# Two chunks of the w3·w_out product in float32r from split parts, and a new order of batch 0's softmax among the weight conversions

## Chip, cores and metric

One core of a Trainium2 chip runs the kernel. The metric is the device time of one execution in microseconds; the time before is a median of three runs. All times inside a run come from one profiled execution, counted from the start of its span. TensorE is called PE, VectorE DVE, ScalarE ACT, SyncE SP.

## The reference

Eight batches, eight heads, 512 tokens and 32 state rows of 64 values each. Attention runs both ways, tokens over state rows and state rows over tokens, each with its own softmax; the two results are put below each other, and heads are laid side by side to rows of 512. Those 4,352 rows go through a bilinear layer:

```python
scores = scale * np.matmul(x, state.transpose(0, 1, 3, 2))
a = softmax(scores)                      # tokens: 512 x 32 a head
xread = np.matmul(a, state)
scores2 = scale * np.matmul(state, x.transpose(0, 1, 3, 2))
a2 = softmax(scores2)                    # state rows: 32 x 512 a head
sread = np.matmul(a2, x)
x = rows of xread and sread              # (8*544) x 512
h = (x @ w1) * (x @ w2) @ w3
out = h @ w_out
```

w1 and w2 are 512x1024, w3 is 1024x1024, w_out 1024x512. The weights come as float64.

## The kernel before

The two last products are joined: the kernel computes wo = w3 @ w_out once (1024x512) and then, for every row, (x@w1 * x@w2) @ wo. Since attention's result is a weighted sum of state rows, w1 and w2 are first multiplied by the state of each batch (per_head, L148); these products, split into a high and a low float32r part, are the `sw_hi` and `sw_lo` tiles. stage1_sums (L312) multiplies them with the attention weights `at_hi` and `at_lo` in three terms (lo·hi, hi·hi, hi·lo), hidden (L299) multiplies the two halves and splits the result into `g_hi` and `g_lo`, and stage2 (L339, L332) multiplies by wo. Batch 0 goes in this plain form; batches 1 to 7 go through quarter_batch (L518), which does the last product in quarters with combined weights; state_rows (L675) does the state rows at the end.

This case is about the prologue, in which the weights are loaded and turned into float32, and batch 0's softmax is computed beside it.

**Conversion.** to_f32 (L103) turns one tile of 128x1024 float64 into float32. SP loads it into `raw` (three places). ACT makes two passes: the high words (L119, into the output) and the low words (L127, into `ulps`, two places; in the first two chunks DVE does this, L123). After a `yield` DVE shifts (L131) and adds (L135). A load into a place of `raw` waits until ACT's second pass of the tile three loads earlier is done.

**Tiles in order.** Eight chunks `w34_k` (half w_out, half the first four row blocks of w3) are converted into places of `w_sb`; w34_first (L568) multiplies each into four PSUM sums, four float32 matmuls a chunk, which the profile shows as eight records. Tiles 4 to 7 of w3 (`convert_w3`, L576) follow, each for one further sum of eight float32 matmuls (w34, L580); their outputs `w3` have two places, so tile 6 waits until PE has used tile 4, and tile 7 until tile 5. finish (L561) splits a sum into wo: a cast on ACT (L98), a subtraction on DVE (L99). Eight halves of w1 and w2 are converted too (convert_half, L588): the first four before, the other four after the first stage1. The second four overwrite places that hold w_out.

**Batch 0's softmax** is the generator scores (L180): it is advanced with `go(softmax)` between conversions. Its steps before: the scores on PE; transposing (L191), the state side's maxima (L194, L195) and exponentials on ACT (L205, two, with their sums), the token side's maxima, subtraction and exponential (L214, L215, L218); the sums and reciprocals (L220 to L226); the transposing back and the split into `at` (L231); last the transposing of the state side's exponentials (L238) into the tile `work`, from which SP's sixteen DMAs of move_blocks (L168, L172) build the tile that read_state (L244) multiplies.

**What sets the order.** PE and SP issue in the order of the code all along. In the prologue, until `order.close()` (L643), ACT and DVE do too; behind it a scheduler places their instructions, those of hidden with priority. Each engine works through its instructions in order, so one that waits holds up all behind it. sets (L592) is two units of per_head for a quarter of the weights; a pair of PSUM banks (`two_banks`) has three places, taken in turn by the w34 pair, the scores of batch 0, the units, and the sums of stage 1.

Of the kernel before, what the change touches and what calls it, by code (L numbers as in the profile page):

```python
# [29 lines left out]
P = 128  # L30
# [6 lines left out]
PLAIN = 1  # L37

@with_exitstack
def attn_bilinear_kernel(  # L40
# [62 lines left out]
    def to_f32(pool, src, out, ends=(NW,), loads=(), wout=None):  # L103
# [12 lines left out]
        for part in parts:  # L116
# [4 lines left out]
            )  # L121
            if len(parts) > 1:
# [53 lines left out]
    def attention_steps(b):  # L176
# [3 lines left out]
        def scores():  # L180
# [15 lines left out]

            first, second = (maxima, turn) if b > PLAIN else (turn, maxima)
            with tc.issue_after(first().ins):
                second()
# [3 lines left out]
            for kt in range(KT):  # L203
                one = slice(kt, kt + 1)
                nc.scalar.activation(  # L205
                    out=e2[:, kt], in_=ps[:, kt], func=AF.Exp, bias=m2[:, one], scale=SCALE, accum_out=sum2[:, one]
                )
            if b > PLAIN:
                yield
# [4 lines left out]
            nc.vector.tensor_reduce(out=m1, in_=s1v, axis=AX.X, op=ALU.max)  # L214
            nc.vector.tensor_tensor(  # L215
                out=s1v, in0=s1v, in1=m1.unsqueeze(2).broadcast_to([P, J, NS]), op=ALU.subtract
            )
            nc.scalar.activation(out=s1, in_=s1, func=AF.Exp, scale=SCALE)  # L218
            yield
            nc.vector.tensor_scalar_add(sum2, sum2, 1e-9)  # L220
            nc.vector.reciprocal(out=sum2, in_=sum2)
# [9 lines left out]
            nc.vector.transpose(out=flat(at), in_=flat(s1))  # L231
            at_tiles[b] = [att.tile([P, KT, S], F32R, name=f"at_{part}", bufs=1) for part in ("hi", "lo")]
            last = split(*at_tiles[b], at)
            yield

# [317 lines left out]
    with tc.tile_pool(name="pro", bufs=2) as pro:  # L553
# [7 lines left out]
        def finish(i):  # L561
            split(wo["hi"][:, i], wo["lo"][:, i], w34_ps[i][:, :DO])

        def convert_first(k):
            ends = PARTS.get(k, (NW,))
            return to_f32(pro, w34_k[k], chunks[k], ends, (), wout=w_out[k])

        def w34_first(k):  # L568

            for i in range(FT // 2):  # L570
# [5 lines left out]
        def convert_w3(i):  # L576
            w3s[i] = pro.tile([P, NW], F32, name="w3", bufs=2)
            return to_f32(pro, w3t[i - FT // 2], w3s[i])
# [31 lines left out]
        for k in range(FT + AHEAD):  # L610
            run([partial(convert_first, k) if k < FT else partial(convert_w3, k - FT // 2)])
            if k >= AHEAD:
                w34_first(k - AHEAD)
        load_x(0)
# [137 lines left out]
```

## Time and profile before

| | |
|---|---|
| median of three runs | 491.09 us (490.76 to 491.37) |
| the profiled execution's own time | 490.61 us |
| its span, first to last instruction | 488.8 us |
| busy: PE, DVE, ACT | 481.6, 391.1, 235.3 us |
| bytes moved by DMA | 52.49 MB |
| mean granted PE clock | 1.000 |

A row of the timeline gives start, length, engine, line, operation, output and inputs, sizes and count; in brackets how long the engine was idle before it, and what released it. "PEld" is the loading of the stationary operand, "SPq" the issuing of DMAs by SP, "issue" time in which nothing visible was waited for. Matmuls overlap, so the interval between two starts tells more than a row's length. Some matmul records are missing in a trace.

### The profile page before, as it was taken

What the parts mean: (1) busy time and instruction counts of PE and PEld (TensorE: products, weight loads), DVE (VectorE), ACT (ScalarE), POOL (GpSimd) and SP (SyncE); (2) the same over time, 40 slices, a digit from 0 to 9 for tenths busy, and PEclk for the clock granted to TensorE, in tenths of its full rate; (3) what the DMA queues carried; (4) which work ended last, traced back from release to release, by engine and by line L of the source; (5) the groups of instructions that cost most, each with busy time, mean ns of one, the idle gap of its engine ahead of it and who ended that gap; (6) DMA issues with size and microseconds to landing.
All of it is one profiled execution on the core that took longest, in us unless ns stands there. A gap on an engine that the chain in (4) does not pass through costs nothing.

```text
span 488.8 us, 8607 instructions
## 1 busy us (share of the span) xinstructions
PE 481.6 (99%) x3390; PEld 368.9 (75%) x3390; DVE 391.1 (80%) x576; ACT 235.3 (48%) x364; POOL 0.2 (0%) x4
## 2 busy tenths in 40 slices
PE   8999999999999999999999999999999999999996
PEld 5444467768688878887888788877977797899885
DVE  5669897699999679958995899599859985678870
ACT  4777784453547044704570556055515541353640
POOL 0000000000000000000000000000000000000000
PEclk9999999999999999999999999999999999999999
DMA  8996981153105404130413041305230223001101
GB/s 341 356 365 251 370 306 27 17 205 90 21 6 196 108 9 171 43 99 4 180 39 94 4 181 41 90 5 180 44 87 5 89 47 84 6 2 43 45 1 44
DMA packets 56361, 52.49 MB, mean 107 GB/s; under 512 B 42752, under 2 KB 50944, under 8 KB 51712
## 3 DMA queue, kind: packets, MB, share of 16 engines
q1 hardware_dynamic: 47488, 43.27, 27.0%
q10 hardware_dynamic: 8832, 8.65, 5.2%
q8 instruction: 27, 0.44, 0.4%
q14 instruction: 14, 0.11, 0.1%
HBM read 38.27 MB, written 8.91 MB: 97 GB/s over the span
## 4 chain that ended last, share of the span: by engine, by line
PE 78%; DVE 11%; ACT 5%; DMA 3%; SPq 2%; issue 1%; ACTq 0%; DVEq 0%
PE ps L321 29%; PE ps_o L436 11%; PE ps L448 8%; PE ps L148 6%; PE ps_o L441 5%; PE ps L453 4%; PE ps L690 3%; PE ps_o L571 3%; PE ps L571 3%; PE ps_o L335 2%; SPq L172 2%; DMA raw<-in_w_dram 2%; PE ps L692 2%; ACT ulps L127 2%; PE ps_o L253 1%; DVE raw L383 1%
## 5 line engine op out<-in xcount | busy, mean ns | idle before, releaser
L321 PE MATMUL ps<-at_lo,sw_hi 128*128 128x512 f32 x256 | 101.3, 396 | 0.1
L321 PE MATMUL ps<-at_hi,sw_lo 128*128 128x512 f32 x256 | 99.8, 390 | 0.0
L321 PE MATMUL ps<-at_hi,sw_hi 128*128 128x512 f32 x256 | 99.7, 389 | 0.0
L525 ACT COPY tmp<-ps 128x512 f32<-128x512 f32 x56 | 32.8, 585 | 118.1 <-PE ps L321 118.1
L321 PEld LDWEIGHTS ps<-at_lo,sw_hi 128*128 128x128 f32 x256 | 48.1, 188 | 16.4 <-DVE g_lo L99 5.0
L321 PEld LDWEIGHTS ps<-at_hi,sw_lo 128*128 128x128 f32 x256 | 48.1, 188 | 10.3
L321 PEld LDWEIGHTS ps<-at_hi,sw_hi 128*128 128x128 f32 x256 | 48.1, 188 | 9.6 <-issue 0.2
L464 DVE TENSOR_TENSOR tmp<-tmp,ps 128x512 f32<-128x512 f32 x42 | 28.8, 687 | 18.4 <-PE ps L453 17.5
L405 DVE TENSOR_TENSOR g_x<-tmp,ps 128x512 f32<-128x512 f32 x28 | 18.9, 676 | 26.3 <-ACT tmp L525 26.3
L98 ACT CAST g_hi<-raw 128x512 fp32r<-128x512 f32 x42 | 24.6, 618 | 31.9 <-DVE raw L405 23.6
L99 DVE TENSOR_TENSOR sw_lo<-ps,sw_hi 128x1024 fp32r<-128x1024 f32 (+1 forms) x34 | 38.0, 1146 | 1.5 <-ACT sw_hi L98 1.5
L436 PEld LDWEIGHTS ps_o<-t,g_hi 128*128 128x128 f32 x224 | 27.8, 191 | 5.0 <-issue 5.0
L148 PE MATMUL ps<-w_sb,st 64*32 64x512 f32 (+1 forms) x544 | 31.4, 570 | 0.0
L98 ACT CAST sw_hi<-ps 128x1024 fp32r<-128x1024 f32 (+1 forms) x34 | 31.0, 967 | 0.1
L98 ACT CAST g_hi<-g_x 128x512 fp32r<-128x512 f32 x42 | 25.4, 626 | 11.3 <-DVE g_x L405 6.4
L436 PE MATMUL ps_o<-t,g_hi 128*128 128x256 f32 x224 | 29.7, 286 | 0.0
L99 DVE TENSOR_TENSOR g_lo<-raw,g_hi 128x512 fp32r<-128x512 f32 x42 | 27.9, 679 | 2.2 <-PE ps_o L441 1.6
L436 PE MATMUL ps_o<-wo,g_hi 128*128 128x256 f32 x224 | 29.1, 283 | 0.0
L436 PEld LDWEIGHTS ps_o<-wo,g_hi 128*128 128x128 f32 x224 | 28.3, 192 | 0.5
L584 PE MATMUL ps_o<-w_sb,w 128*128 128x512 f32 x64 | 28.5, 599 | 0.0
L99 DVE TENSOR_TENSOR g_lo<-g_x,g_hi 128x512 fp32r<-128x512 f32 x42 | 27.1, 681 | 1.8 <-PE ps_o L441 1.8
L448 PE MATMUL ps<-t,g_hi 128*128 128x512 f32 x112 | 28.0, 392 | 0.0
(103 smaller groups left out, 784.5 us busy)
## 6 DMA issues: line engine op xcount, KB each, us to landing
raw<-in_w_k_dram SPq DMA_DIRECT2D x8, 1024.0 KB, 6.8
x_d<-in_x_d_dram SPq DMA_DIRECT2D x8, 1024.0 KB, 6.8
raw<-in_w_dram SPq DMA_DIRECT2D x8, 1024.0 KB, 6.7
x_s<-in_x_s_dram SPq DMA_DIRECT2D x8, 1024.0 KB, 5.1
out_dram<-tmp ACTq DMA_DIRECT2D x56, 128.0 KB, 1.8
raw<-in_w3t_dram SPq DMA_DIRECT2D x4, 1024.0 KB, 7.4
e<-work SPq DMA_DIRECT2D x112, 32.0 KB, 2.0
sread<-turned SPq DMA_DIRECT2D x128, 4.0 KB, 1.7
```

What stands on the lines that cost most here:

```text
L98: nc.scalar.copy(out=hi, in_=src),
L99: nc.vector.tensor_tensor(out=lo, in0=src, in1=hi.bitcast(F32), op=ALU.subtract),
L148: nc.tensor.matmul(ps[j * NS:(j + 1) * NS, q], sts[b][rows, j], moving(rows, j), start=True, stop=True)
L321: nc.tensor.matmul(ps[:, i], w[:, kt, c:c + P], a[:, kt], start=(k == 0), stop=(k == 3 * KT - 1))
L436: nc.tensor.matmul(ps[:, tt * HO:(tt + 1) * HO], g, w(part, k), start=(fresh and k == 0 and tt == 0 and part == "lo"), stop=False, skip_gr ...
L441: nc.tensor.matmul(ps[:, tt * HO:(tt + 1) * HO], g, w("hi", k), start=False, stop=(k == QF - 1), skip_group_check=True)
L448: nc.tensor.matmul(ps[:, tt].rearrange("p (n d) -> p n d", n=2), g, w(k), start=(k == 0), stop=False, skip_group_check=True,)
L453: nc.tensor.matmul(ps[:, tt, :HO], g, w(k)[:, 0], start=False, stop=(k == QF - 1), skip_group_check=True)
L464: sum2 = lambda out, x, y: nc.vector.tensor_tensor(out=out, in0=x, in1=y, op=ALU.add)
L525: copied = nc.scalar.copy(out=a_sb, in_=ps[:, 0])
L571: nc.tensor.matmul(w34_ps[i][:, :DO], chunks[k][:, DO + i * P:DO + (i + 1) * P], w_out[k], start=(k == 0), stop=(k == FT - 1),)
L584: nc.tensor.matmul(w34_ps[i][:, :DO], w3s[i][:, k * P:(k + 1) * P], w_out[k], start=(k == 0), stop=(k == FT - 1))
```

## The change

Three edits of the prologue, all in the code that orders it.

First, chunks 4 and 6 (`SPLIT`) are multiplied in float32r: their two halves are split into high and low parts (`split_of`), into tiles of the `sw` pool, and w34_first makes three matmuls instead of one for each of the four sums. The split is called by to_f32 of the following chunk, between ACT's first and second pass. In the same way finish(0) now runs between the passes of w3 tile 5.

Second, scores yields in smaller steps for batch 0: the transposing and the token side come first, the state side's maxima, exponentials and sums come in a step of their own, after the split into `at`. The order of the conversions becomes: w3 tile 6, w12 half 1, half 2, w3 tile 7, half 3, half 4 (before: half 1, half 2, tile 6, tile 7, half 3, half 4, by the order of their loads).

Third, w3 tiles 6 and 7 are converted into a pair of tiles of the `sw` pool and don't wait for PE's use of tiles 4 and 5.

```diff
+SPLIT = (4, 6)
...
-    def to_f32(pool, src, out, ends=(NW,), loads=(), wout=None):
+    def to_f32(pool, src, out, ends=(NW,), loads=(), wout=None, between=None):
...
                 out=out[:, part], in_=high.bitcast(F32), func=AF.Prelu, scale=2.0**-112, alpha=-(2.0**32)
             )
+            if between:
+                between()
...
+            if b < PLAIN:
+                turn()
+                yield
+                token_side()
+            else:
...
             last = split(*at_tiles[b], at)
             yield
+            if b < PLAIN:
+                maxima()
+                state_side()
+                nc.vector.tensor_scalar_add(sum2, sum2, 1e-9)
+                nc.vector.reciprocal(out=sum2, in_=sum2)
+                yield
...
+            def both():
+                halves[k] = sw_pair()
+                for n, src in enumerate((w_out[k], chunks[k][:, DO:])):
+                    split(*(t[:, n] for t in halves[k]), src)
...
+            if k in SPLIT:
+                hi, lo = halves[k]
+                for i in range(FT // 2):
+                    cols = slice(i * P, (i + 1) * P)
+                    for a, b in ((hi, hi), (hi, lo), (lo, hi)):
+                        nc.tensor.matmul(w34_ps[i][:, :DO], a[:, 1, cols], b[:, 0], start=False, stop=False)
+                return
...
+        def convert_w3(i, between=None):
+            if i < FT - 2:
+                w3s[i] = pro.tile([P, NW], F32, name="w3", bufs=2)
+            else:
+                if not spare:
+                    spare.extend(t.rearrange("p k f -> p (k f)").bitcast(F32) for t in sw_pair())
+                w3s[i] = spare.pop(0)
...
-        go(w1_0), go(softmax), go(w1_0)
+        go(softmax)
+        go(w3_6), go(softmax), go(w3_6)
+        go(w1_0), go(w1_0)
+        go(softmax)
         finish(4)
-        go(w2_0), go(w3_6), go(softmax), go(w3_6)
+        go(w2_0), go(w2_0)
         w34(5)
+        go(w3_7), go(softmax), go(w3_7), go(softmax)
+        finish(5)
+        go(w1_1), go(w1_1)
         go(softmax)
...
```

What this does to the engines' orders is shown at three places. The first is ACT at chunks 5 to 7 (each has its own `raw`: 162 is chunk 5's in both kernels). Before:

```order
L119 ACTIVATE w_sb_90<-raw_162 128x1024
L127 ACTIVATE ulps_163<-raw_162 128x1024
L119 ACTIVATE w_sb_90<-raw_174 128x1024
L127 ACTIVATE ulps_175<-raw_174 128x1024
L119 ACTIVATE w_sb_90<-raw_186 128x1024
L127 ACTIVATE ulps_187<-raw_186 128x1024
```

And after (line numbers are those of the changed kernel):

```order
L120 ACTIVATE w_sb_90<-raw_162 128x1024
L99 CAST sw_hi_166<-w_sb_90 128x512 x2
L130 ACTIVATE ulps_163<-raw_162 128x1024
L120 ACTIVATE w_sb_90<-raw_180 128x1024
L130 ACTIVATE ulps_181<-raw_180 128x1024
L120 ACTIVATE w_sb_90<-raw_200 128x1024
L99 CAST sw_hi_204<-w_sb_90 128x512 x2
L130 ACTIVATE ulps_201<-raw_200 128x1024
```

The casts of chunks 4 and 6 stand behind the first pass and ahead of the second pass of chunks 5 and 7. The second place is DVE at the third and fourth w12 half and the first two units of `sets` (shift and add of one half: TENSOR_SCALAR and ISA on `w_sb`; `ps_2_346` is the first unit's sum before, `ps_2_374` after). Before:

```order
L99 TENSOR_TENSOR wo_93<-ps_o_292,wo_93 128x512
L131 TENSOR_SCALAR w3_311<-w3_311 128x1024
L135 ISA w3_311<-w3_311,ulps_313 128x2048
L131 TENSOR_SCALAR w_sb_90<-w_sb_90 128x1024
L135 ISA w_sb_90<-w_sb_90,ulps_320 128x2048
L131 TENSOR_SCALAR w_sb_90<-w_sb_90 128x1024
L135 ISA w_sb_90<-w_sb_90,ulps_327 128x2048
L99 TENSOR_TENSOR sw_lo_345<-ps_2_346,sw_hi_344 128x2x256
```

And after:

```order
L100 TENSOR_TENSOR wo_93<-ps_o_317,wo_93 128x512
L134 TENSOR_SCALAR w_sb_90<-w_sb_90 128x1024
L138 ISA w_sb_90<-w_sb_90,ulps_342 128x2048
L197 TENSOR_REDUCE m2_281<-ps_2_258 128x2
L198 TENSOR_SCALAR m2_281<-m2_281 128x2
L256 TENSOR_SCALAR sum2_283<-sum2_283 128x2
L257 RECIPROCAL sum2_283<-sum2_283 128x2
L134 TENSOR_SCALAR w_sb_90<-w_sb_90 128x1024
L138 ISA w_sb_90<-w_sb_90,ulps_355 128x2048
L100 TENSOR_TENSOR sw_lo_373<-ps_2_374,sw_hi_372 128x2x256
```

The maxima and sums of the state side, with the two exponentials of ACT between them, moved from the start of the softmax to between these two halves; w3's tile 7 moved ahead. The third place is DVE at the first two hidden products (L303 before, L327 after, of the sums `ps_2_406` and `ps_2_426` before, `ps_2_434` and `ps_2_454` after) and the transposing of the exponentials. Before:

```order
L135 ISA w_sb_90<-w_sb_90,ulps_468 128x2048
L303 TENSOR_TENSOR tmp_421<-tmp_421,ps_2_406 128x512
L303 TENSOR_TENSOR tmp_441<-tmp_441,ps_2_426 128x512
L99 TENSOR_TENSOR g_lo_420<-tmp_421,g_hi_419 128x512
L99 TENSOR_TENSOR g_lo_440<-tmp_441,g_hi_439 128x512
L238 STREAM_TRANSPOSE work_478<-e2_261 128x1024
```

And after:

```order
L327 TENSOR_TENSOR tmp_449<-tmp_449,ps_2_434 128x512
L138 ISA w_sb_90<-w_sb_90,ulps_496 128x2048
L100 TENSOR_TENSOR g_lo_448<-tmp_449,g_hi_447 128x512
L327 TENSOR_TENSOR tmp_469<-tmp_469,ps_2_454 128x512
L100 TENSOR_TENSOR g_lo_468<-tmp_469,g_hi_467 128x512
L262 STREAM_TRANSPOSE work_506<-e2_282 128x1024
```

The add of the last w12 half moved behind the first product, and the second product behind the first low part.

More of the change, by code (lines that the diff above doesn't have):

```diff
@@ L616, in attn_bilinear_kernel @@
         softmax = scores()
-        next(softmax)
-        finish(0)
+        w1_0, w2_0, w1_1, w2_1 = map(convert_half, range(4))
+        go = lambda steps: next(steps, None)
+        w3_6, w3_7 = convert_w3(6), convert_w3(7)
+        go(softmax)
         finish(1)
```

68 lines of the change are left out of this document (38 added, 30 removed).

## The prediction

> **What bounds the kernel now.** First the page: busy time by engine and the engines of the chain that ended last.
>
> ```profile
> span 488.8 us, 8607 instructions
> PE 481.6 (99%) x3390; PEld 368.9 (75%) x3390; DVE 391.1 (80%) x576; ACT 235.3 (48%) x364; POOL 0.2 (0%) x4
> PE 78%; DVE 11%; ACT 5%; DMA 3%; SPq 2%; issue 1%; ACTq 0%; DVEq 0%
> ```
>
> PE is busy all along, yet a fifth of the chain lies elsewhere. The table by stretches says where a second engine is as full (columns: window, sum, busy time and count of each engine, clock, DMA share, GB/s).
>
> ```profile
> 40.00:60.00 20.00, 19.95 (x77) 8.50 (x76) 18.10 (x24) 15.10 (x19) 0.00 (x0) 1.00 0.78 288
> 100.00:120.00 20.00, 19.95 (x182) 14.53 (x181) 19.45 (x31) 9.46 (x12) 0.00 (x0) 1.00 0.49 162
> 200.00:300.00 100.00, 100.00 (x805) 82.08 (x804) 84.63 (x121) 45.30 (x76) 0.00 (x0) 1.00 0.25 77
> ```
>
> In the stretches shown before 120 us DVE is 90% busy and more beside a full PE: two engines each without room. Later PE alone is full. The chain in order of time shows how the first part hands over to the rest (start, length, what):
>
> ```profile
> 76.69 1.15 DVE work L238
> 78.43 0.18 SPq L172
> ...
> 90.28 1.25 DVE work L191
> ...
> 133.22 0.58 DVE g_x L405
> 133.85 11.19 PE ps L321 x48
> ```
>
> Batch 0's turned state exponentials (L238) are moved by sixteen DMAs in SP's queue; batch 1's first transpose (L191) waits for them, since it takes their buffer; DVE runs nearly full from there to 133 us, where PE waits for it. From 133.85 on PE has no wait that matters. So the end moves as far as 133.85 moves, and that hangs on when L238 runs, unless PE is later still.
>
> **1. The matmuls of two chunks.** PE in the first stage, with one interval of a three-term product (first and last of a run of 35 matmuls on 128x512 float32r):
>
> ```profile
> 22.00 1.88 PE L571 MATMUL ps_o<-w_sb 128*128 128x512 f32 x4
> 25.43 1.88 PE L571 MATMUL ps_o<-w_sb 128*128 128x512 f32 x4
> 35.82 1.09 PE L148 MATMUL ps<-x_d,st 64*32 64x512 f32 x16
> 63.47 1.09 PE L148 MATMUL ps<-w_sb,st 64*32 64x256 f32 x32
> 67.40 0.39 PE L321 MATMUL ps<-at_hi,sw_hi 128*128 128x512 f32 x1
> 75.13 0.39 PE L321 MATMUL ps<-at_hi,sw_lo 128*128 128x512 f32 x1
> ```
>
> A chunk takes 25.43 - 22.00 = 3.43 us; by (75.13 - 67.40)/34 = 0.227, twelve float32r matmuls take 2.73. That is 0.70 less a chunk, 1.4 in all, if the parts are ready. The splits run on ACT and DVE between conversions; ACT around them:
>
> ```profile
> 20.12 1.15 ACT L119 ACTIVATE w_sb<-raw 128x1024 f32<-128x1024 f32 x1 [1.61 <-DMA raw<-in_w_k_dram]
> 21.18 1.15 ACT L127 ACTIVATE ulps<-raw 128x1024 int32<-128x1024 uint32 x1
> 29.74 1.13 ACT L119 ACTIVATE w<-raw 128x1024 f32<-128x1024 f32 x1 [2.51 <-DMA raw<-in_w3t_dram]
> 32.20 1.16 ACT L119 ACTIVATE w<-raw 128x1024 f32<-128x1024 f32 x1 [0.28 <-DMA raw<-in_w3t_dram]
> 34.30 1.06 ACT L98 CAST wo<-ps_o 128x512 fp32r<-128x512 f32 x2
> 40.76 0.69 ACT L205 ACTIVATE e<-ps,m 128x512 f32<-128x512 f32 x1 [1.27 <-DVE m L195]
> 42.01 0.20 ACT L205 ACTIVATION_READ_ACCUMULATOR e<-ps,m 128x1 f32 x1
> 59.86 1.05 ACT L98 CAST sw_hi<-ps 128x512 fp32r<-128x512 f32 x2
> 64.10 1.19 ACT L119 ACTIVATE w_sb<-raw 128x1024 f32<-128x1024 f32 x1 [0.62 <-DMA raw<-in_w_dram]
> 68.10 1.13 ACT L119 ACTIVATE w_sb<-raw 128x1024 f32<-128x1024 f32 x1 [0.80 <-DMA raw<-in_w_dram]
> 72.73 1.06 ACT L302 COPY tmp<-ps 128x512 f32<-128x512 f32 x2
> ```
>
> Chunk 4's casts stand behind chunk 5's first pass, which waits for its DMA until 20.12: they run from 21.18 to 22.25 (1.06 for two, row 34.30), and DVE subtracts to about 23.05. PE gets to chunk 4 at 22.0 and its third matmul needs the second low part: 23.05 + 10 x 0.227 = 25.3, against 25.43 before. Chunk 4 gains nothing. Chunk 6 is reached some 3.4 us later and its parts are done at about 28.8, just as PE comes: it gains 0.7. So PE is 0.7 ahead at 35.8, not 1.4.
>
> **2. Loads.** The second pass of chunks 5 and 7 (the last reader of `raw`) now stands behind two casts, and SP's next loads wait for it:
>
> ```profile
> 22.36 0.33 SPq L115 DMA_DIRECT2D raw<-in_w3t_dram  x1
> 24.83 0.33 SPq L115 DMA_DIRECT2D raw<-in_w3t_dram  x1
> ```
>
> They are issued at about 23.4 and 25.5, 1.1 and 0.7 later. In before these tiles landed at 29.7 and 32.2 (ACT's waits above); since one landing also follows the other, they may land as before or 1.1 later. I take 0.5 later, 32.7 for tile 5; the ends are 32.2 and 33.5. finish(0) goes between its two passes and adds a cast of 0.5.
>
> **3. DVE until the last conversion that PE needs.** DVE's rows:
>
> ```profile
> 34.43 1.23 DVE L135 CUSTOM_DVE_ANT_0 w<-w,ulps 128x2048 uint16<-128x2048 uint16 x1 [0.34 <-ACT ulps L127]
> 35.57 1.28 DVE L99 TENSOR_TENSOR wo<-ps_o,wo 128x512 fp32r<-128x512 f32 x2
> 53.10 1.22 DVE L99 TENSOR_TENSOR at_lo<-work,at_hi 128x1024 fp32r<-128x1024 f32 x1 [1.11 <-ACT at_hi L98]
> 60.63 0.69 DVE L131 TENSOR_SCALAR w_sb<-w_sb 128x1024 int32<-128x1024 int32 x1
> 61.46 1.23 DVE L135 CUSTOM_DVE_ANT_0 w_sb<-w_sb,ulps 128x2048 uint16<-128x2048 uint16 x1
> 62.60 1.28 DVE L99 TENSOR_TENSOR sw_lo<-ps,sw_hi 128x512 fp32r<-128x512 f32 x2
> 76.61 1.24 DVE L238 STREAM_TRANSPOSE work<-e 128x1024 f32<-128x1024 f32 x1
> 90.28 1.25 DVE L191 STREAM_TRANSPOSE work<-ps 128x1024 f32<-128x1024 f32 x1 [1.72 <-DMA work<-work]
> ```
>
> Before, from tile 5's add (34.43) to the end of the fourth w12 half's add (61.46 + 1.23 = 62.69) are 28.26 us, of which 1.11 are idle and 0.64 are finish(0)'s subtract (half of row 35.57), which now comes earlier. The same work is 26.5 us, and DVE is full, so moving steps among each other wins nothing. After: tile 5's first pass at 32.7, 33.75 finish(0)'s cast, 34.3 its subtract (0.64), 34.95 the shift (61.46 - 60.63 = 0.83), 35.75 the add. Now the maxima and the two exponentials stand ahead of the fourth half: its shift and add (62.69 - 60.63 = 2.06) come last, the rest, 24.4 us, ends with the maxima at about 60.15. Then the two engines take turns: two exponentials on ACT (42.01 + 0.20 - 40.76 = 1.45) to 61.6, and only behind them, since ACT works in order, the half's two passes (1.06 + 1.15) to 63.85; then the add, 1.23: 65.1, which is 2.4 later than before. In before the same exponentials stood in front of steps that PE did not need for long. What hides this ping-pong would be a conversion already passed by ACT; the new order has none there.
>
> **4. PE's wait.** The second unit of the fourth row of the PE view reads that half, and its PSUM place is freed by the first low part of row 62.60 (0.64), which now follows the add: 65.7. Before it began half of 1.09 behind 63.47, at 64.0. So PE stands still for about 2.4 us at 63 and is 1.7 late instead of 0.7 early. Nothing else is queued on PE that could fill this, since its order is fixed.
>
> **5. ACT up to the first hidden product.** From the casts of row 59.86 to the first copy of row 72.73 are 12.87 us, 0.62 and 0.80 of it waits for DMA: 11.45 of work, all of it still behind the fourth half's second pass, which ACT leaves at 63.8. The copy comes at 75.25, 2.5 late. The waits for DMA are gone, since most loads are issued earlier; that is the gain of the new spacing, and it is smaller than the turn-taking.
>
> **6. The transposed exponentials.** From that copy to L238 are 76.61 - 72.73 = 3.88 us. The new DVE order puts the last half's add between the first product and its low part, and the second product behind that: copy 0.6, product 0.6, add 1.2, low part 0.6, product 0.7, cast 0.6, low part 0.6, together 4.9 (each by the rows of its kind above). L238 at 80.1; the same steps laid along before's own rows come out 0.2 late, so 79.9, 3.3 late. The second product also frees PE's next PSUM place, so PE is some 2.5 late there.
>
> **7. To the end.** L238 to L191 is a chain of SP's sixteen moves and one landing, 90.28 - 76.61 = 13.67 us, unchanged: L191 is 3.3 late too, and by the window of 100 to 120 us DVE has 0.55 us in 20 to catch up. Less about 0.4 for that and for tile 5 landing earlier than I take, the sum is **+2.9 us**. The profiled execution took 490.61 (span 488.8 and 1.81 around it), so its like would take 493.5; against the median of 491.09, which is 0.48 above it, I predict **494.0 us**. Without the extra 0.5 of tile 5 the same walk gives 2.5, with tile 5 at 33.5 it gives 3.8. What float32r parts cost ACT and DVE themselves (four casts, four subtracts) lies in waits for DMA like that of row 20.12, and costs only through parts 1 and 2.
>
> [...]
>
> **Rivals.**
>
> *PE is the only bound (faster).* The conversions stay ahead of PE, as in before, where the fourth half was done at 62.69 and PE came at 63.47. Then PE keeps what part 1 gives, 0.7 to 1.4 us: at best 491.09 - 1.4 = 489.7. It decides at one point: the fourth half's add must end by 63. For it speaks that before shows hardly a PE wait; against it that DVE would have to win 2 us in a stretch in which it has 1.11 of idle time. [...] 0.11.
>
> *The lateness is caught up (no change).* L191 waited 1.72 us before, so the chain through SP has no more cover than that of DVE; but if PE, itself late, lets DVE close its gaps between 90 and 133 us and the exponentials meet an idle ACT earlier than I think, the end moves by under 1 us: 491.5. 0.09.
>
> *The loads come later too (slower still).* Tile 5 at 33.5 or later, because three loads are issued 0.7 to 1.8 us later in a row: +3.8 to +4.3, 495.1. For it speaks the wait of 2.51 us for tile 4 in before, against it that tile 5 landed 2.46 us behind tile 4, as if the loads were served in turn. 0.08. In this case PE would stand still for over 3 us. [...]
>
> **How the numbers follow.** My forecast, 493.3 to 494.9, has 0.72. 0.2% is 1.0 us, about what a measurement of this kernel can tell from no change. Faster by more than that: 0.11; within it: 0.09; slower: 0.72 + 0.08 = 0.80. The range from 491.9 to 495.6 leaves out the faster case and most of the unchanged one, and the tail of late loads.
>
> **What would show it.** In the profile after: chunk 4's third matmul near 23, no gain there; PE's view with a wait of 2 to 3 us for DVE near 63, before the second of the narrow units; ACT's two exponentials near 60 with idle time before them; the first hidden copy near 75, L238 near 80, L191 near 93.5, and the last PE wait of the first part near 136.7. Wrong it would be if the fourth half's add ended by 63, if DVE idled more than 2 us between 36 and 59, or if L191 came before 91.

## The result and the profile after

The changed kernel takes 493.4 us (median of six runs, 493.01 to 494.18), the kernel before 490.92 us in the same series (490.71 to 491.37): a ratio of 1.0051, with a 95% interval of 1.0040 to 1.0062, or 2.5 us more. The profiled execution took 493.64 us, with a span of 491.9 us and a mean granted clock of 0.997. Names and lines below are those of each run's own kernel; in the changed one the moved lines are L262 (transposing the state exponentials, L238 before), L194 (batch 1's transpose, L191), L120 and L130 (the two passes on ACT), L134 and L138 (shift and add on DVE), L327 (hidden product), L615 and L612 (chunks unsplit and split), L151 (per_head) and L635 (w3 tiles).

The page, first the busy time of each engine, then the chain that ended last:

```profile
PE 481.8 (98%) x3398; PEld 370.2 (75%) x3398; DVE 393.4 (80%) x580; ACT 237.1 (48%) x368; POOL 0.2 (0%) x4
...
PE 83%; DVE 8%; DMA 4%; ACT 2%; SPq 2%; issue 1%; DVEq 0%; ACTq 0%
```

Busy shares tell nothing of the loss; PE even shows 0.2 us more than before, although two chunks need less of it (the slow matmuls below, by estimate half of 3.4 us, fill that up). The chain's share of PE rose from 78 to 83%, that of DVE fell from 11 to 8%. Where it leads is read from the chain in order of time (start, length, what):

```profile
60.45 0.86 ACT e L207 x3
...
62.23 1.19 ACT ulps L130
63.42 0.02 issue
63.44 1.23 DVE w_sb L138
64.67 0.61 DVE sw_lo L100
65.28 0.04 issue
65.32 1.11 PE ps L151 x16
66.43 3.97 PE ps_o L635 x6
70.40 8.21 PE ps L345 x36
```

It passes from ACT's exponentials over the fourth w12 half (ACT's pass, DVE's add) and the first low part to PE, one step behind the other with under 0.1 us between them: the turn-taking that the prediction described. From 65.32 to 103 us it stays on PE. On DVE one sees it as idle time with ACT as the releaser, three times in a row (idle time in brackets):

```profile
58.41 1.21 DVE L197 TENSOR_REDUCE m<-ps 128x2 f32<-128x1024 f32 x1
...
61.34 0.17 DVE L256 TENSOR_SCALAR sum<-sum 128x2 f32<-128x2 f32 x1 [1.51 <-ACT e L207]
...
62.37 0.69 DVE L134 TENSOR_SCALAR w_sb<-w_sb 128x1024 int32<-128x1024 int32 x1 [0.66 <-ACT w_sb L120]
63.44 1.23 DVE L138 CUSTOM_DVE_ANT_0 w_sb<-w_sb,ulps 128x2048 uint16<-128x2048 uint16 x1 [0.38 <-ACT ulps L130]
...
75.13 0.69 DVE L327 TENSOR_TENSOR tmp<-tmp,ps 128x512 f32<-128x512 f32 x1 [0.25 <-ACT tmp L326]
...
79.45 1.24 DVE L262 STREAM_TRANSPOSE work<-e 128x1024 f32<-128x1024 f32 x1
...
93.08 1.25 DVE L194 STREAM_TRANSPOSE work<-ps 128x1024 f32<-128x1024 f32 x1 [1.43 <-DMA work<-work]
```

The fourth half's add ends at 63.44 + 1.23 = 64.67 (62.69 before), the exponentials are transposed at 79.45 (76.61), batch 1's transpose comes at 93.08 (90.28). PE, at the places shown of before:

```profile
25.76 1.88 PE L615 MATMUL ps_o<-w_sb 128*128 128x512 f32 x4
...
35.49 1.09 PE L151 MATMUL ps<-x_d,st 64*32 64x512 f32 x16
...
62.82 0.66 PE L151 MATMUL ps<-w_sb,st 64*32 64x256 f32 x16
65.32 1.11 PE L151 MATMUL ps<-w_sb,st 64*32 64x256 f32 x16 [1.84 <-DVE sw_lo L100]
...
91.52 1.09 PE L151 MATMUL ps<-x_d,st 64*32 64x512 f32 x16
```

The last of these rows is, in the trace of before:

```profile
88.43 1.09 PE L148 MATMUL ps<-x_d,st 64*32 64x512 f32 x16
```

PE is 0.33 us ahead at batch 0's scores (35.49 against 35.82), stands still for 1.84 us before 65.32, and is 91.52 - 88.43 = 3.09 us late at batch 1's scores. Right behind the stop it is only some 1.3 us late. The table by stretches shows where the rest comes from, in its clock column, the third from the right:

```profile
63.00:65.00 2.00, 0.48 (x16) 0.00 (x1) 1.62 (x3) 2.00 (x5) 0.00 (x0) 1.00 0.28 41
65.00:67.00 2.00, 1.68 (x17) 0.73 (x18) 2.00 (x4) 2.00 (x3) 0.00 (x0) 0.60 0.90 360
67.00:69.00 2.00, 2.00 (x4) 0.72 (x3) 1.82 (x3) 2.00 (x4) 0.00 (x0) 0.55 0.70 213
69.00:71.00 2.00, 2.00 (x8) 1.15 (x7) 1.86 (x4) 2.00 (x3) 0.00 (x0) 1.00 1.01 426
```

Behind the stop the granted clock is one half for some 3.4 us: the windows from 65 to 69 us mix it with full speed (0.60 and 0.55), and in steps of half a microsecond it is 0.90 from 65.0 to 65.5, 0.50 from there to 68.5, 0.69 to 69.0 and then 1.00. The six records of tile 7 take 3.97 us (chain above), where before they took 2.84.

### The profile page after: what moved, and what is told of

Its sections match the earlier page's. It is cut to its first block, busy times and chain, and to the rows that moved or that the text cites. A ratio compares the mean times of both kernels' runs of the same rounds, so it can differ in the third digit from the quotient of the medians.

```text
span 491.9 us, 8624 instructions
## 1 busy us (share of the span) xinstructions
PE 481.8 (98%) x3398; PEld 370.2 (75%) x3398; DVE 393.4 (80%) x580; ACT 237.1 (48%) x368; POOL 0.2 (0%) x4
## 4 chain that ended last, share of the span: by engine, by line
PE 83%; DVE 8%; DMA 4%; ACT 2%; SPq 2%; issue 1%; DVEq 0%; ACTq 0%
PE ps L345 35%; PE ps_o L460 11%; PE ps L472 8%; PE ps L151 7%; PE ps_o L465 5%; PE ps L477 4%; PE ps_o L359 4%; DMA raw<-in_w_k_dram 3%; PE ps L744 3%; SPq L175 2%; PE ps L746 2%; PE ps_o L277 1%; DVE sw_lo L100 1%; DVE w_sb L138 1%; PE ps_o L635 1%
## 5 line engine op out<-in xcount | busy, mean ns | idle before, releaser
L151 PE MATMUL ps<-w_sb,st 64*32 64x512 f32 (+1 forms) x544 | 32.1, 577 | 1.8 <-DVE sw_lo L100 1.8
L120 ACT ACTIVATE w_sb<-raw 128x1024 f32<-128x1024 f32 (+3 forms) x18 | 18.8, 1057 | 9.2 <-DMA raw<-in_w_k_dram 9.2
```

What stands on the lines that cost most here:

```text
L151: nc.tensor.matmul(ps[j * NS:(j + 1) * NS, q], sts[b][rows, j], moving(rows, j), start=True, stop=True)
```

## The experiments

All were measured beside the kernel before, whose medians were 490.91, 490.72, 490.90 and 490.87 us in the four series (e1 to e4, e5 to e8, e9 to e11, e12). The table sets the median of each against that of its series, and beside it the profiled execution's span and three times in its trace. "Later" is the larger of two delays against before: that of PE's batch-1 scores (88.43 before) and that of batch 1's transpose on DVE (90.28 before).

| run | us against before | span | exponentials transposed | PE's batch-1 scores | batch 1's transpose | later | span against before |
|---|---|---|---|---|---|---|---|
| before | 0 | 488.8 | 76.61 | 88.43 | 90.28 | 0 | 0 |
| after | +2.5 | 491.9 | 79.45 | 91.52 | 93.08 | 3.09 | 3.1 |
| e1 no split | +3.2 | 493.0 | 79.89 | 90.80 | 94.04 | 3.76 | 4.2 |
| e2 maxima early | +1.7 | 492.6 | 78.15 | 89.03 | 92.38 | 2.10 | 3.8 |
| e3 tile 7 whole | +2.8 | 492.0 | 79.39 | 90.28 | 93.53 | 3.25 | 3.2 |
| e4 state side first | +4.1 | 493.3 | 80.57 | 92.87 | 94.22 | 4.44 | 4.5 |
| e5 state side behind tile 6 | +1.3 | 490.4 | 77.29 | 88.94 | 91.68 | 1.40 | 1.6 |
| e6 = e2, products paired | -0.4 | 489.0 | 76.82 | 88.03 | 90.70 | 0.42 | 0.2 |
| e7 = e3, turned early | +2.4 | 491.1 | 72.62 | 90.89 | 92.09 | 2.46 | 2.3 |
| e8 = e6, turned early | +0.2 | 488.8 | 70.98 | 88.46 | 89.65 | 0.03 | 0 |
| e9 before, split alone | -1.0 | 488.8 | 76.34 | 88.23 | 90.39 | 0.11 | 0 |
| e10 = e9, three chunks | +0.8 | 490.4 | 78.05 | 89.50 | 91.94 | 1.66 | 1.6 |
| e11 = e7, PE kept busy | +2.1 | 491.7 | 73.16 | 91.34 | 92.54 | 2.91 | 2.9 |
| e12 = e5, products paired | -0.1 | 489.8 | 76.58 | 89.39 | 90.59 | 0.96 | 1.0 |

In eleven of the thirteen the span moved by the later of the two delays within 0.22 us: there, what happens behind 93 us adds next to nothing, and two paths share the end. (The two others are e1, 0.4 off, and e2, whose profiled execution was the longest of its runs and had a mean granted clock of 0.83 from 130 to 140 us; its median is the better number.) Most medians lie below the span's shift, e2's by 2.1 us and the others by up to 1 us. The profiled execution of before, 490.61 us, was 0.1 to 0.3 us under the medians of before, and those of e1 and e9 were 0.7 us above their own medians. So a difference of half a microsecond between two traces says little.

**e1, the split alone taken away.**

```diff
-SPLIT = (4, 6)
+SPLIT = ()
```

> The changed kernel with chunks 4 and 6 left in float32, all else as changed. My theory (the state side's maxima and exponentials between the third and fourth w12 half make ACT and DVE take turns, and that delays L238 and with it the end): the split parts win PE 0.3 us and cost nothing else, so without them finish(0)'s cast comes 0.3 us later and the time is 0.0 to 0.5 us over the changed kernel's, that is 2.5 to 3.0 us over before; PE still waits about 2 us near 63. Rival (the four casts, which hold up the second passes and so the loads, are what costs): back to within 0.7 us of before.

Measured: 494.07 us (493.88 to 494.76), ratio 1.0067 (1.0055 to 1.0079). Without split parts the kernel is 0.7 us slower than the changed one, a little more than the 0.0 to 0.5 expected. The split is no part of the loss; the casts that it adds to ACT cost less than it gives.

**e2, the maxima as a step of their own, early.** The state side's maxima stand ahead of the third half, so that DVE has long taken them when ACT comes to the exponentials, which stay ahead of the fourth.

```diff
             if b < PLAIN:
                 maxima()
+                yield
                 state_side()
...
         finish(5)
+        go(softmax)
         go(w1_1), go(w1_1)
         go(softmax)
```

> The changed kernel with one step cut in two: the state side's maxima on DVE go ahead of the third w12 half's shift, the exponentials stay on ACT behind that half's passes. My theory: the exponentials are then ready to run when ACT gets to them (maxima done near 57.7 instead of 59.8, ACT's exponentials by 59.2 instead of 61.3), the fourth half's add ends near 62.7 instead of 64.7, PE's wait near 63 falls from 1.8 to under 0.5 us, L238 starts near 77.5 instead of 79.45, and the time is 0 to 1 us over before (1.5 to 2.5 us under the changed kernel). Rival (the split's casts cost it): within 0.7 us of the changed kernel. Second rival (PE's wait and its slow clock behind it set the end, not L238): also near before, with L238 still late.

Measured: 492.63 us (492.21 to 494.41), ratio 1.0032 (1.0020 to 1.0044). The turn-taking went: the fourth half's add ended at 62.43, PE did not stop near 63, and the clock stayed at 1.00 there. But 1.7 us remained, more than expected. DVE shows where, from the first hidden product on:

```profile
74.20 0.68 DVE L328 TENSOR_TENSOR tmp<-tmp,ps 128x512 f32<-128x512 f32 x1
75.56 0.69 DVE L100 TENSOR_TENSOR g_lo<-tmp,g_hi 128x512 fp32r<-128x512 f32 x1 [0.69 <-ACT g_hi L99]
...
78.15 1.24 DVE L263 STREAM_TRANSPOSE work<-e 128x1024 f32<-128x1024 f32 x1
```

The first product now comes at 74.20, as early as before (74.02), and the transposing 3.95 us behind it, where before it took 2.59: product, wait for the cast, low part, second product, wait, low part.

**e3, tile 7 multiplied in one place.**

```diff
-LAST = 5
+LAST = 8
...
-        w34(7, range(LAST, FT))
```

> The changed kernel with tile 7's three last matmuls moved ahead of the two units of the second quarter on PE, so that PE has 2.6 us of work while the fourth half is converted. My theory: PE's wait near 63 goes (to under 0.5 us) and PE comes to the first stage-1 sum near 67.0 instead of 70.2, but ACT and DVE are as late as before, L238 stays within 0.7 us of 79.45, and the time stays 1.8 to 2.8 us over before. Rival (PE's wait, and the half clock of 65 to 69 us, set the end): the 3 us come back, the time is within 0.7 us of before, though L238 is as late.

Measured: 493.68 us (492.8 to 496.95), ratio 1.0064 (1.0043 to 1.0086). The stop near 63 was gone, one of 1.84 us came before 71.28 instead, PE's scores were 1.85 us late instead of 3.09, and the time did not fall; the exponentials were transposed at 79.39, as late as in the changed kernel. So the loss does not hang on PE's stop alone.

**e4, the state side back at the start of the softmax.**

```diff
             if b < PLAIN:
-                turn()
+                with tc.issue_after(turn().ins):
+                    maxima()
+                state_side()
+                token_side()
                 yield
-                token_side()
...
-            if b < PLAIN:
-                maxima()
-                state_side()
...
```

> The changed kernel with the state side (maxima, exponentials, sums) back at the start of batch 0's softmax; split parts, the new order of the conversions and the places of tiles 6 and 7 stay. My theory: no turn-taking between the third and fourth half; the fourth half's add ends near 62.7, PE doesn't wait there, L238 is within 1 us of before's 76.6, and the time is 0.7 us under to 0.8 us over before. Rival (the split's casts or the new order of conversions cost it): still 1.5 to 2.5 us over before.

Measured: 494.97 us (494.12 to 495.1), ratio 1.0079 (1.0067 to 1.0091): the worst of all, and missed. It was not the undoing that it was meant to be. ACT's three exponentials now stood ahead of tile 6's passes, which in the kernel before stood behind conversions that ACT had already done. DVE, then PE:

```profile
45.23 0.69 DVE L134 TENSOR_SCALAR sw_hi<-sw_hi 128x1024 int32<-128x1024 int32 x1 [2.14 <-ACT sw_hi L120]
```

```profile
53.79 8.66 PE L630 MATMUL ps_o<-w_sb,sw_hi 128*128 128x512 f32 x16 [3.07 <-DVE wo L100]
```

The same turn-taking, 2.14 us at 45, became a stop of PE of 3.07 us at 54. It supports the mechanism (ACT's place in the order, not the softmax's amount of work) but says nothing on the state side's late place; e5 was made for that.

**e5, the state side behind tile 6's first passes.** As in e4, with the two exponentials a step later, so that ACT has passed tile 6 when it comes to them.

```diff
             if b < PLAIN:
-                turn()
+                with tc.issue_after(turn().ins):
+                    maxima()
                 yield
+                state_side()
                 token_side()
...
```

> The clean undo of the moved state side, which e4 was not: the two maxima are taken right behind the turning of the scores, and ScalarE's two exponentials stand behind tile 6's first passes as they did before; the divisors follow at the next step. Split parts and tile 7's two places stay. Theory (the four waits of VectorE between 60 and 65 us come from the state side's late place): the add of the fourth w1 half ends at 62.6 to 63.2 us, TensorE does not stop for 1.84 us at 63 us and its clock stays at 1.00, the product m0 is ready near 74 us; of the loss of 2.5 us there remain 0.5 to 1.7 us, since tile 7's second place still puts the two first hidden products one behind the other (e2 kept 1.7 us for that reason). Rival (what moved is only where ScalarE and VectorE take turns, and 43 to 48 us is as bad a place as 60 to 65): VectorE loses 1.5 us or more near 45 us again and the time stays at +2.5 us or more.

Measured: 492.0 us (491.42 to 494.12), ratio 1.0031 (1.0020 to 1.0043). As the theory had it, and a little earlier: the fourth half's add ended at 62.0, PE did not stop near 63, the first product came at 73.34, and 1.3 us remained. Beside the serial products a stop of PE of 0.97 us before 51.39 is left.

**e6, e2 with the first two hidden products back to back** (both copies, both products, then both low parts, as before).

```diff
+    def hidden_pair(sums, n, gs):
+        tiles = [main.tile([P, NF], F32, name="tmp", bufs=4)[:, :n] for _ in sums]
+        with tc.high_priority():
+            for a_sb, ps in zip(tiles, sums):
+                copied = nc.scalar.copy(out=a_sb, in_=ps[:, 0, :n])
+            for a_sb, ps in zip(tiles, sums):
+                product = nc.vector.tensor_tensor(out=a_sb, in0=a_sb, in1=ps[:, 1, :n], op=ALU.mult)
+            with tc.issue_after(copied.ins), tc.issue_after(product.ins):
+                for a_sb, g in zip(tiles, gs):
+                    last_split[:] = split(*g, a_sb)
...
```

> e2 (the maxima as a step of their own, early) and beside it the first two hidden products made back to back: both copies, both products, then both low parts, as the order of before had them. Theory (after e2 the whole rest of the loss is the serial order of the two products, 3.95 us from the first product to the transposing against 2.59 before): the transposing of the state exponentials starts near 76.8 us, against 78.15 in e2 and 76.6 before, and the time is before's plus 0 to 0.5 us (490.9 to 491.4). Rival (the loss of e2 has another place, such as TensorE's waits at 69 to 71 us): the transposing comes earlier but the time stays 1.3 us or more above before.

Measured: 490.31 us (489.79 to 491.87), ratio 0.9991 (0.9982 to 1.0001). The loss is gone, a little more than expected. DVE at the place shown for e2:

```profile
74.24 1.28 DVE L337 TENSOR_TENSOR tmp<-tmp,ps 128x512 f32<-128x512 f32 x2
75.61 1.29 DVE L100 TENSOR_TENSOR g_lo<-tmp,g_hi 128x512 fp32r<-128x512 f32 x2
76.82 1.24 DVE L263 STREAM_TRANSPOSE work<-e 128x1024 f32<-128x1024 f32 x1
```

Same first product (74.24 against 74.20), but the casts of one product now run under the other, and the transposing comes 2.58 us behind it instead of 3.95. By the medians this took 2.1 us off e2, all of its 1.7 us of loss and 0.4 more; the interval of the ratio just reaches 1, so e6 is not shown to be faster than before.

**e7, e3 with the exponentials transposed ahead of the hidden products.**

```diff
         finish(7)
+        go(softmax)
         order.close()
...
-                with tc.issue_after(last_split[1].ins):
-                    go(softmax)
+                go(softmax)
```

(and a `yield` between the transposing and the moves, which keep their place).

> e3 (tile 7 in one place) and beside it the transposing of the state exponentials moved ahead of the first hidden product; the moves that follow it keep their place in the order. It tells whether the chain transposing, moves, reading of the state sets the end (theory), or TensorE's own lateness (rival). Theory: the transposing starts at 72 to 75 us instead of 79.4, the wait for the state's blocks is over by 91.5 us at the latest, and the loss falls from 2.8 us to 1.3 to 1.9 us, which is how late TensorE's scores of batch 1 were in e3 (1.85 us): 492.3 to 492.8 us. Rival: TensorE sets the end already, so the time stays within 0.3 us of 493.7.

Measured: 493.14 us (492.83 to 493.54), ratio 1.0050 (1.0037 to 1.0063). Neither number came: 2.4 us remained where the theory had 1.3 to 1.9, and the rival no change. The wait for the state's blocks was indeed gone, and PE released batch 1's transpose:

```profile
92.09 1.25 DVE L194 STREAM_TRANSPOSE work<-ps 128x1024 f32<-128x1024 f32 x1 [1.06 <-PE ps L151]
```

But PE was 2.46 us late instead of e3's 1.85. In the profiled execution it had stopped for 2.21 us before 70.66 and ran at half clock behind that, which e3 with 1.84 us did not. First e7, then e3, PE's row at the stop; then the window of 71 to 73 us in e7 and in e3:

```profile
70.66 0.80 PE L347 MATMUL ps<-at_lo,sw_hi 128*128 128x512 f32 x1 [2.21 <-DVE sw_lo L100]
```

```profile
71.28 0.50 PE L345 MATMUL ps<-at_lo,sw_hi 128*128 128x512 f32 x1 [1.84 <-DVE sw_lo L100]
```

```profile
71.00:73.00 2.00, 2.00 (x6) 1.52 (x6) 1.78 (x4) 2.00 (x4) 0.00 (x0) 0.50 1.00 422
```

```profile
71.00:73.00 2.00, 1.72 (x7) 1.43 (x8) 1.78 (x4) 2.00 (x4) 0.00 (x0) 1.00 1.03 418
```

The half clock is not what held e7 up, though. The profiled execution, with a mean clock of 0.996 over its span, was the fastest of the five (492.83 us); the other four, with 0.999 or 1.000, took 492.95 to 493.54. What e7 left in place is the turn-taking near 60 us: its first hidden product comes at 74.88, against 74.02 in before.

**e8, e6 with the exponentials transposed early**, by e7's edit of the transposing.

> e6 and beside it the early transposing of e7: maxima early, the two products back to back, the state exponentials transposed ahead of them. Theory: the chain through the state no longer sets the end at all and TensorE does, 0.6 us later than before at its batch-1 scores in e2; the time is before's minus 0.5 to plus 0.7 us (490.4 to 491.6), and at most 0.3 us from e6. Rival (the wait for the state's blocks was worth more than the chain shows, or the split parts' gain of 0.6 us now comes through): 490.2 us or less, a kernel faster than before.

Measured: 490.87 us (490.2 to 491.07), ratio 0.9996 (0.9987 to 1.0005). Within the theory's range of times, though 0.56 us above e6 where at most 0.3 was expected. The ranges of e6 and e8 overlap, so e8 is not shown to be slower; transposing 5.8 us earlier than e6 wins nothing, at any rate. PE releases batch 1's transpose then, and ahead of 76.31 it waits 0.31 us for a hidden product, which it does not in e6. That the moved step delays this product is argued from the order.

**e9, the kernel before with the split alone.** `SPLIT`, `split_of` and the float32r products of w34_first, called between the passes as in the change; nothing else of it.

> The kernel before with one part of the change alone: chunks 4 and 6 multiplied from split float32r parts; the softmax, the order of the tiles and the buffers of tiles 6 and 7 as before. Theory (e1 against the changed kernel: the split is worth about 0.6 us whatever stands behind it, since TensorE and the w3 tiles are a little earlier): before minus 0.3 to minus 0.8 us (490.1 to 490.6), with TensorE's scores of batch 0 0.2 to 0.5 us earlier. Rival (TensorE is not what the first 35 us wait for, the casts cost as much as they give, and the 0.6 us of e1 come from how the split falls into the changed order): before plus or minus 0.2 us.

Measured: 489.93 us (489.35 to 491.11), ratio 0.9983 (0.9974 to 0.9992): 1.0 us below before by the medians, 0.8 by the ratio. It is the fastest of all, 3.5 us below the changed kernel. The interval leaves a gain of 0.4 to 1.3 us. In its profiled execution PE's scores of batch 0 come at 35.63, 0.19 us ahead, a little under what was expected. That execution was one of the longer ones of its kernel (490.62 us, with the span of before's), so the trace does not show where the gain lies.

**e10, e9 with a third chunk.**

```diff
-SPLIT = (4, 6)
+SPLIT = (2, 4, 6)
```

> e9 with a third chunk, number 2, in split parts: one more chunk of 12 float32r products of about 0.23 us for 4 float32 ones that took about 3.4 us together, and two more casts and subtractions of 128 x 1024 in all on ScalarE and VectorE. Theory (the gain follows TensorE's work): 0.2 to 0.4 us less than e9. Rival (ScalarE and VectorE bound these chunks, so further casts only cost): 0.3 to 1.5 us more than e9.

Measured: 491.68 us (490.61 to 494.81), ratio 1.0018 (1.0003 to 1.0033), 1.75 us above e9. The rival was right, with a quarter of a microsecond more than its range. PE is no longer ahead in the first stage and then waits for what the other engines or the loads deliver late:

```profile
36.26 1.09 PE L151 MATMUL ps<-x_d,st 64*32 64x512 f32 x16 [0.49 <-DMA x_d<-in_x_d_dram]
37.58 14.00 PE L607 MATMUL ps_o<-w_sb,w 128*128 128x512 f32 x32 [0.23 <-DVE wo L100]
51.95 7.13 PE L607 MATMUL ps_o<-w_sb,w 128*128 128x512 f32 x16 [0.37 <-DVE w L138]
```

The gain of two splits is not a rate per chunk: as far as these rows tell, only so much of it can be had as fits beside the conversions.

**e11, e7 with eight products that nobody reads in PE's stop.**

```diff
+            if quarter == 0:
+                acc.append(bank())
+                hi = at_tiles[0][0]
+                for n in range(8):
+                    nc.tensor.matmul(acc[0], hi[:, 0, :P], hi[:, 0], start=True, stop=True)
             stage1(0, 2 * quarter + 1, gs)
...
```

(and `early_stage2` takes only one more bank, since the first is there already).

> e7 and eight float32r products that nobody reads, into a bank that is empty, in the 2.21 us in which TensorE waits near 69 us (their sums are overwritten; no result changes). It tells what the halved clock behind that stop costs. Theory (the clock falls because TensorE stands still, and in e7 TensorE's lateness sets the end): the granted clock stays at 1.00 from 70 to 74 us, where e7 had 0.50 to 0.58, TensorE's scores of batch 1 come 0.6 to 1.6 us earlier than e7's 90.89, and the time falls by 0.3 to 1.5 us against e7. Rival (the clock falls for another reason, such as a schedule of its own or the DMA traffic): 0.50 is granted again and the time is e7's within 0.3 us. Third (the clock stays up but what follows waits for VectorE's products anyway): clock 1.00 and the time within 0.3 us of e7.

Measured: 492.99 us (492.7 to 493.65), ratio 1.0041 (1.0028 to 1.0053), within 0.2 us of e7: by clock and time the third case. The window of 71 to 73 us and PE's rows:

```profile
71.00:73.00 2.00, 1.94 (x9) 1.51 (x9) 1.79 (x4) 2.00 (x4) 0.00 (x0) 1.00 1.05 428
```

```profile
69.16 1.97 PE L714 MATMUL ps_o<-at_hi 128*128 128x512 f32 x8
...
79.21 1.09 PE L151 MATMUL ps<-w_sb,st 64*32 64x512 f32 x16 [1.27 <-DVE tmp L329]
```

The clock stayed at 1.00 where e7's trace has 0.50, while the loads ran at nearly the same rate (428 and 422 GB/s): at this rate both clocks were granted. That the filling kept the clock up is not shown: all five executions have a mean clock of 0.999 or 1.000, but so have four of e7's five, in which nothing was filled. What e11 and those four show together is that at a mean clock of 0.999 or 1.000 the times are much the same (492.70 to 493.65 us, and 492.95 to 493.54). In e11 PE came to the first unit behind stage 1 earlier than in e7 (76.85 against 77.91) and then waited 1.27 us for a hidden product. Its scores of batch 1 did not come earlier (91.34 against 90.89); but the profiled execution was 0.9 us behind e7's at batch 0's scores already.

**e12, e5 with the products back to back**, by e6's edit.

> e5 (state side back behind tile 6's first passes) and beside it the first two hidden products back to back as in e6: of the change there stay the split parts, the own places of tiles 6 and 7 with tile 7's passes early, and the steps of the softmax in their new order among the conversions. It closes the sum. Theory (the late state side and the two products one behind the other are the whole loss, and the rest of the change is the gain of the split): the transposing of the state exponentials starts at 75.7 to 76.2 us (e5's 77.29 less 1.3), and the time is before's minus 0.5 to minus 1.2 us (489.7 to 490.4), like e9's minus 1.0. Rival (own places and the new order of the steps cost something of their own): before minus 0.2 us or more (490.7 us up), although the transposing comes before 76.6 us.

Measured: 490.82 us (490.01 to 491.55), ratio 0.9993 (0.9984 to 1.0002). The medians give the rival (-0.1 us), the ratio lies between the two. The pair took 1.2 us off e5, as expected, and the transposing came at 76.58. What remains against e9 is PE's:

```profile
51.85 7.13 PE L646 MATMUL ps_o<-w_sb,sw_hi 128*128 128x512 f32 x16 [1.17 <-DVE wo L100]
```

PE stands still for 1.17 us ahead of tile 6, and its batch-1 scores are 0.96 late. That the two exponentials ahead of the w12 halves cause it is argued from the order, not shown alone: e4 and e5, which have them early too, also stop there (3.07 and 0.97 us), and e6, which has them later, does not.

## Why the prediction was right

The forecast was 494.0 us and slower; 493.4 was measured. The sum gave 2.9 us: by the medians it was 2.5, by the two profiled executions 493.64 - 490.61 = 3.03. By its steps:

1. *Matmuls.* Chunk 6 gave what was worked out: chunk 7 starts at 31.96, where before it was 32.30, and chunks 5 and 6 together take 6.20 us instead of 6.87. Chunk 4, taken to gain nothing, lost 0.33 (chunk 5 starts at 25.76, before at 25.43):

```profile
22.53 0.50 PE L612 MATMUL ps_o<-sw_hi 128*128 128x512 f32 x1 [0.41 <-ACT sw_hi L99]
22.87 0.39 PE L612 MATMUL ps_o<-sw_lo,sw_hi 128*128 128x512 f32 x1
23.34 0.50 PE L612 MATMUL ps_o<-sw_hi,sw_lo 128*128 128x512 f32 x1
...
31.96 1.88 PE L615 MATMUL ps_o<-w_sb 128*128 128x512 f32 x4
```

   PE waited 0.41 us for the casts, and its third matmul started at 23.34, not near 23.05, since the second low part was done only at 23.28. So PE was 0.33 ahead at the scores instead of 0.7. That the split parts give more than they cost ACT and DVE held (e1, e9), but only for as many as fit (e10).

2. *Loads.* Tile 5 was taken at 32.7 and came at 31.32, below even the lower end:

```profile
28.96 1.14 ACT L120 ACTIVATE w<-raw 128x1024 f32<-128x1024 f32 x1
...
31.32 1.16 ACT L120 ACTIVATE w<-raw 128x1024 f32<-128x1024 f32 x1 [0.19 <-DMA raw<-in_w3t_dram]
33.02 0.59 ACT L99 CAST wo<-ps_o 128x512 fp32r<-128x512 f32 x1 [0.55 <-PE ps_o L615]
```

   Tile 4 had landed before ACT came, although its load was issued a microsecond later than in before. Half of the 1.4 us was lost again: finish(0)'s cast waited 0.55 us for PE, ahead of tile 5's second pass, and the add came at 35.07 instead of the 35.75 taken. So this was the term that was mis-sized most, by 0.7 us in effect; the sum's allowance of 0.4 covered over half of it. It was not one lucky execution: in the nine other runs with this order of the stage (e2 to e8, e11, e12) ACT came to tile 5 between 30.69 and 32.41. The rival with later loads fell.

3. *Turn-taking.* The add of the fourth half ended at 64.67 against 65.1. Right, and the 0.4 comes from step 2.

4. *PE's wait.* The second unit began at 65.32 against 65.7, after a stop of 1.84 us (2.4 taken). But PE then lost further in the profiled execution: it was some 1.3 us late at 65.3 and 3.1 late at batch 1's scores. In between the granted clock was 0.50 for 3.4 us, by estimate 1.7 of these 1.8 us. The sum had no such term, and its 2.5 us of lateness behind the hidden products was short by 0.6. The loss does not need the half clock: of the six executions of the changed kernel the one with a mean clock of 1.000 took 493.01 us, still 2.1 us over before.

5. *First hidden copy.* At 74.43 instead of 75.25: 1.7 us late, not 2.5, for step 3's 0.4 and since ACT had 0.4 less to do than taken.

6. *Transposing.* At 79.45 against 79.9; from the copy 5.02 us against 4.9. Right, and e2, e5, e6 and e12 show that the serial order of the two products is a cause of its own, which stays when the turn-taking is gone: pairing the products took 2.1 us off e2 and 1.2 off e5.

7. *The end.* From the transposing to batch 1's transpose 13.63 us (13.67 before). But the prediction let the end hang on this chain alone "unless PE is later still", and in the profiled execution PE was: 3.09 us against 2.80. The chain of that execution runs over PE from 65.32 to 103 us, and not over the transposing and its moves. Both paths were late by nearly the same, so that taking away one alone could win little: e3 (PE 1.2 us earlier) and e7 (the wait for the moves gone) remained at +2.8 and +2.4. PE comes to the place of row 133.85 of before at 136.94, where 136.7 was expected, so nothing was caught up by then; the rival *the lateness is caught up* fell.

The mechanism was thus the one forecast, turn-taking near 60 us that makes the add, the hidden products and the transposing late. That the size fits so well is in part luck: PE won 0.33 us at the matmuls instead of 0.7, tile 5 came 1.4 us earlier than taken, and the half clock was not in the sum.

Of the change's parts, the one that cuts PE's work gains 0.8 to 1.0 us alone (e9), well under the 1.4 us of matmul work that the prediction worked out for it, and by the difference the rest of the change, which moves the two other engines' work, lost 3.5 us. The rival *PE is the only bound* failed at the point that it named: the add had to end by 63 and ended at 64.67.

What stays open: e6 and e12 are 0.6 and 0.9 us above e9 (each against its own series; the interval of e6 overlaps that of e9). Whether the own places of tiles 6 and 7 give or cost anything was not tried by itself, and the stop in e12 is only part of an answer.

## What to carry to other kernels

When two engines in fixed order hand work back and forth, price a moved step by who stands behind it on both: the state side's maxima and exponentials made the conversion behind them 2.0 us later (62.69 to 64.67), not by their work, which was there before too, but because ACT had to wait for DVE's maxima with the exponentials and with the next tile's passes behind them. With the maxima taken a step earlier (e2) the add ended at 62.43. Put such a pair where the other engine has a finished tile in hand, and issue products that need each other's engines in pairs, so that one's cast runs under the other's product (this took 2.1 us off e2 and 1.2 off e5). And test the parts of a change apart: the one that gained was worth some 1 us alone and was hidden under a loss of 3.5.

## What the runs showed of the hardware

At some stops of PE of about 2 us and more the granted clock fell to one half, in some executions of a kernel and not in others. The traces of after, e7 and e4 each have a stretch at 0.50 of some 3.4 us, at stops of 1.84, 2.21 and 3.07 us. It begins between 0.3 us before the end of the stop (e4, with 0.74 from 53 to 54 us and the stop's end at 53.79) and 0.1 us behind it (after). In e2 the window from 130 to 140 us has 0.83, what 3.4 us at one half would give; there PE had begun again at 128.88, behind a DMA that landed at 128.75. A window from e4's:

```profile
54.00:56.00 2.00, 2.00 (x3) 0.97 (x4) 1.86 (x3) 0.00 (x0) 0.00 (x0) 0.50 1.00 418
```

The clock stayed at 1.00 at stops of 1.84 us (e3, 69 to 75 us) and 1.86 us (e1, 62 to 70 us). That of e1 stands at the same place in the order as that of after, between the same matmuls. How often it happens can be estimated from the mean clock of each execution: 3.4 us at one half take 0.0035 off the mean over a span of 490 us, and the traces of these four runs have 0.996 or 0.997, those of the others 0.998 or more. Of the executions, 0.997 or less came in three of six of the changed kernel, one of five of e1, one of six of e2, two of six of e3, two of ten of e5, one of five of e7, one of eleven of e10, in all five of e4, whose stop is the longest, and in no other. In e7 the slow stretch cost nothing that the times show, as far as one execution tells. Where it comes late it may: e2's profiled execution, with 0.83 from 130 to 140 us, was 1.7 us longer than any other of its kernel.

When a load is issued says little here about when it lands. Tiles 4 and 5 of w3 were issued at 23.54 and 25.62 in the changed kernel instead of 22.36 and 24.83, and were ready by 28.96 and 31.32 instead of 29.74 and 32.20. This is not shown to be an effect of the later issue.
